# Another computed instruction order for the opening of a cross-attention and ReGLU kernel

## Chip, cores, metric

One core of one Trainium2 chip. The metric is device time of the core in microseconds (us), over several executions.

## The reference

```python
def _attn_ref(x, state):                  # x (8,8,512,64), state (8,8,32,64)
    scale = 1.0 / np.sqrt(D)
    a = softmax(scale * x @ state^T);   xread = a @ state
    a2 = softmax(scale * state @ x^T);  sread = a2 @ x
    return np.concatenate([xread, sread], axis=2)

def _moe_ref(x, w_gate, w_val, w_out):    # on 8 x (512 + 32) = 4352 rows of 512
    return (np.maximum(x @ w_gate, 0.0) * (x @ w_val)) @ w_out      # 512 -> 1536 -> 512
```

(The two softmaxes are written out in the original.) The output is (4352, 512) in float32; the kernel multiplies in bf16.

## The kernel before

The kernel never forms `xread`. It multiplies each batch's 32 state rows with both weight matrices (`U`, "state products") and the normalised attention, transposed (`ANS`), with `U`. The state products are *column-tiled*: each of their matmuls has the shape 64x32 in the profile's lines, where the others have 128x128. A *visit* is a group of them between whole ones. The program gives every group of matmuls one of eight PSUM banks, which is free again when ScalarE or VectorE has copied or used what is in it. Per batch the 1536 gate and value columns are 12 *slices* of 128 columns, four 512-column matmuls each. ScalarE takes the relu of a slice's gate half, VectorE multiplies it with the value half, and 12 *output pieces* of four matmuls follow.

```python
def c_unit(b, lo, n):                 # state products of n columns, gate and value
    ps = held["c", b, lo] = [bank("upc")[:, 0:2 * n]... for kc in range(NK)]
    for w in range(2):                # w 0: gate weights, 1: value weights
        u_mm([p[:, w] for p in ps], b, w, lo, n)    # eight 64x32 matmuls
def gv(b, jf):                        # one slice: 2 banks, 4 matmuls
    held["gv", b, jf] = [bank("gv_ps"), bank("gv_ps")], hsb[b][:, jf], S
    for w in range(2):
        for kc in range(NK):
            gv_mm(held["gv", b, jf][0], b, jf, w, kc)   # U x ANS
```

The order of the opening is a string of words. It covers batches 0 and 1, the preparation of batch 2 and the first four slices of batch 2. A word is a step with its arguments; digits after `@` are the PSUM banks; `.act`, `.dve`, `.pool` name the engine. Each engine gets its instructions in the order of the words:

```python
for word in program.split():
    word, _, banks = word.partition("@")
    given.extend(int(n) for n in banks)
    name, *args = word.split(".")
    steps[name](*(int(v) if v.isdigit() else v for v in args))
# then the steady loop:
for g in range(first, NF * (B + 1)):      # first = 2 * 12 + 4
    gv / relu / mult / an output piece, and the units hung on g
```

The words that matter: `spin` filler matmuls on TensorE; `xT`, `xT2` transposes of the input; `sc`, `ex`, `nr`, `nx` scores, exponential (ScalarE), row sums and scaling (VectorE); `aT`, `ao` transposes of the attention (`kc` 0 and 1) and their copies into `ANS`; `c`, `co` state products and their copies into `U`; `u`, `uo` the same 512 columns at a time; `gv`, `re`, `mu` a slice, its relu, its multiply; `o` an output piece; `sr`, `sn` the state read (`a2 @ x`); `dw`, `dx`, `ds`, `do`, `df` loads, `xn` casts, `xp` padded copies, all issued on GpSimd's queue.

The softmax here doesn't subtract the row's maximum and nothing guards it: scores larger than these inputs give would overflow.

## Time and profile before

| | before |
|---|---|
| time, median of 3 runs | 224.15 us (223.98 to 224.34) |
| span of the profiled run | 221.9 us |
| TensorE busy | 96% |
| products of columns 256 to 511: value half starts | 16.10 us, after a wait for weights |
| products of columns 512 to 767 start | 19.04 us |
| first slice of the steady loop starts | 55.72 us |

How to read it: TensorE is nearly full, so time is to be had only where TensorE stands before the steady loop. The last three rows cut the run into three stretches. A change in one stretch shows as a shift of the next mark; if the distance between two marks is the same in two kernels, nothing happened between them. The lines behind the rows are in the prediction.

Some matmul records are missing (x1930 of 1959 on the page before), so "x7" of an eight-matmul group can be a lost record. I compare starts of groups.

### The profile page before, as it was taken

The page shows a single profiled execution, that of the slowest core. Times are in us where ns is not written, and L with a number is a line of the kernel's source. Part 1 is how long each engine was busy: PE and PEld are TensorE (multiplying, and loading weights), DVE is VectorE, ACT ScalarE, POOL GpSimd, SP SyncE. Part 2 cuts the span into 40 slices and gives each one's busy share as a digit, 9 for nine tenths or more (in the row PEclk, how much of TensorE's full clock was granted, in tenths as well). Part 3 has the DMA queues.
Part 4 walks back from the last instruction along what each step waited for, and adds up shares of the span by engine and source line. Part 5 has one row for each costly group of instructions (what it writes and reads, how often), then busy time and mean ns, then how long its engine had stood idle before and what let it go on. Part 6 is the DMA issues. An engine that isn't in the chain of part 4 may idle for free.

```text
span 221.9 us, 4820 instructions
## 1 busy us (share of the span) xinstructions
PE 213.5 (96%) x1930; PEld 106.1 (48%) x1959; DVE 131.0 (59%) x233; ACT 123.3 (56%) x233; POOL 48.9 (22%) x54
## 2 busy tenths in 40 slices
PE   7989999999999999999999999999999999999994
PEld 3544454444544444444444444444444445666544
DVE  3489988965786568664867378646875433222100
ACT  4688788752567555574466456645655444222222
POOL 8867754300603343015000700000000000000000
PEclk9999999999999999999999999999999999999999
DMA  6999999062055862771169114511311112222332
GB/s 155 179 195 196 201 240 284 30 154 84 0 136 200 159 219 75 164 237 52 49 142 282 53 47 98 101 43 47 95 50 47 47 49 50 50 47 54 91 95 95
DMA packets 37879, 25.48 MB, mean 115 GB/s; under 512 B 18944, under 2 KB 33280, under 8 KB 37856
## 3 DMA queue, kind: packets, MB, share of 16 engines
q1 hardware_dynamic: 24992, 16.85, 27.5%
q0 software_dynamic: 11968, 7.47, 21.7%
q10 hardware_dynamic: 896, 0.85, 1.3%
q8 instruction: 15, 0.25, 0.5%
q14 instruction: 8, 0.07, 0.1%
HBM read 18.35 MB, written 8.91 MB: 123 GB/s over the span
## 4 chain that ended last, share of the span: by engine, by line
PE 83%; DMA 12%; POOL 2%; issue 2%; DVE 0%; POOLq 0%; DVEq 0%
PE o_ps L353 38%; PE gv_ps L316 31%; DMA st_f<-in_state_dram 5%; PE gv_ps L333 5%; PE up L291 4%; DMA wv_sb<-in_moe_w_val_dram 4%; DMA xb<-in_x_dram 3%; PE sc_ps L200 1%; PE o_ps L382 1%; PE sr_ps L264 1%; POOL st_b L124 1%; POOL xb L415 0%; PE stT_ps L129 0%; POOL xb L423 0%; PE aT_ps L235 0%
## 5 line engine op out<-in xcount | busy, mean ns | idle before, releaser
L316 PE MATMUL gv_ps<-ans,U 128*128 128x512 bf16 x372 | 93.6, 379 | 1.0 <-ACT ans L249 0.3
L353 PE MATMUL o_ps<-wo_sb,h_sb 128*128 128x512 bf16 x358 | 92.0, 379 | 1.7 <-issue 1.6
L340 ACT ACTIVATE g_sb<-gv_ps 128x512 bf16<-128x512 f32 (+1 forms) x108 | 62.7, 580 | 50.2 <-PE gv_ps L316 37.5
L344 DVE TENSOR_TENSOR h_sb<-gv_ps,g_sb 128x512 bf16<-128x512 f32 x96 | 64.8, 688 | 41.5 <-ACT g_sb L340 40.7
L316 PEld LDWEIGHTS <-U 128*128 128x128 bf16 x384 | 36.0, 98 | 40.7 <-issue 0.9
L353 PEld LDWEIGHTS <-h_sb 128*128 128x128 bf16 x372 | 35.3, 98 | 40.0 <-issue 1.6
L361 ACT COPY o_sb<-o_ps 128x512 f32<-128x512 f32 x29 | 17.1, 590 | 16.2 <-PE o_ps L353 16.2
L301 ACT CAST U<-up 128x512 bf16<-128x512 f32 x37 | 19.2, 594 | 11.1 <-PE up L291 11.1
L301 DVE CAST U<-up 128x512 bf16<-128x512 f32 x35 | 22.1, 683 | 2.3 <-PE up L291 1.9
L142 POOL CAST xb<-xf 128x1024 bf16<-128x1024 f32 x10 | 10.1, 1042 | 55.6 <-DMA xf<-in_x_dram 55.6
L256 POOL COPY xa<-xb 128x2048 bf16<-128x2048 bf16 (+1 forms) x9 | 15.6, 1750 | 12.9 <-issue 12.7
L213 DVE TENSOR_REDUCE cs<-e_sn 128x16 f32<-128x512 bf16 x16 | 10.8, 678 | 8.9 <-ACT e_sn L207 8.9
L344 DVE TENSOR_TENSOR hs_sb<-gv_ps,g_sb 128x256 bf16<-128x256 f32 x12 | 5.1, 425 | 15.3 <-PE gv_ps L333 10.5
L207 ACT ACTIVATE e_sn<-sc_ps 128x512 bf16<-128x512 f32 x16 | 9.7, 604 | 4.5 <-PE sc_ps L200 4.4
L219 DVE TENSOR_TENSOR a_sn<-e_sn,rc 128x512 bf16<-128x512 bf16 x16 | 11.1, 707 | 0.3
L291 PEld LDWEIGHTS <-stT 64*32 64x32 bf16 x512 | 6.0, 90 | 10.0 <-issue 8.7
L311 ACT CAST U<-upc 128x512 bf16<-128x512 f32 (+1 forms) x18 | 8.7, 542 | 1.5 <-PE upc L291 1.5
L291 PE MATMUL up<-wg_sb,stT 64*32 64x512 bf16 x144 | 7.5, 381 | 0.0
L200 PEld LDWEIGHTS <-xT 128*128 128x128 bf16 x128 | 5.6, 98 | 3.7 <-ACT xT L177 0.5
L333 PE MATMUL gv_ps<-br,wg_sb 128*128 128x256 bf16 x48 | 7.2, 273 | 0.1
L333 PE MATMUL gv_ps<-br,wv_sb 128*128 128x256 bf16 x48 | 7.2, 273 | 0.0
L291 PE MATMUL up<-wv_sb,stT 64*32 64x512 bf16 x144 | 7.1, 380 | 0.0
(65 smaller groups left out, 124.0 us busy)
## 6 DMA issues: line engine op xcount, KB each, us to landing
out_dram<-o_sb SPq DMA_DIRECT2D x26, 256.0 KB, 2.4
xf<-in_x_dram SPq DMA_DIRECT2D x4, 1024.0 KB, 6.1
wo_sb<-in_moe_w_out_dram POOLq DMA_DIRECT2D x2, 768.0 KB, 14.4
wg_sb<-in_moe_w_gate_dram POOLq DMA_DIRECT2D x5, 256.0 KB, 9.0
wv_sb<-in_moe_w_val_dram POOLq DMA_DIRECT2D x5, 256.0 KB, 9.7
out_dram<-o_sb SPq DMA_DIRECT2D x10, 128.0 KB, 2.4
xf<-in_x_dram POOLq DMA_DIRECT2D x1, 1024.0 KB, 15.3
xb<-in_x_dram POOLq DMA_DIRECT2D x3, 256.0 KB, 6.1
```

Source lines behind the costliest of these rows:

```text
L142: copy[eng](out=xb[b][:, :, hs].rearrange("p c h d -> p h c d"), in_=xf[b][:, hs])
L213: nc.vector.reduce_sum(out=cs, in_=e_v, axis=AX.X)
L219: {"dve": nc.vector, "pool": nc.gpsimd}[eng].tensor_tensor(out=by_pair(a_sn[b], jp).rearrange("p r (j n) -> p r j n", n=Ns), in0=e_v, in1= ...
L256: nc.gpsimd.tensor_copy(out=v[:, hs:hs + src.shape[1]], in_=src)
L291: nc.tensor.matmul(dst[parity][32 * j:32 * j + 32], stT[r:r + 64, b, j, 32 * parity:32 * parity + 32], wsb[r:r + 64, j, lo:lo + n], start= ...
L301: copy[eng](out=U[b][:, w, kc, lo:lo + 512], in_=held["u", b, w, lo][kc])
L316: nc.tensor.matmul(ps[w], U[b][:, w, kc, f0:f0 + 128], ANS[b][:, kc].rearrange("p c t -> p (c t)"), start=(kc == 0), stop=(kc == NK - 1))
L333: nc.tensor.matmul(ps[w][:, 0:nt], wsb[:, j, f0:f0 + 128], br[:, j].rearrange("p b n -> p (b n)"), start=(j == 0), stop=(j == NJ - 1))
L340: nc.scalar.activation(out=g_sb[:, 0:n], in_=ps[0][:, 0:n], func=AF.Relu)
L344: nc.vector.tensor_tensor(out=dst, in0=ps[1][:, 0:n], in1=held["g", b, jf][:, 0:n], op=ALU.mult)
L353: nc.tensor.matmul(held["o", b, tsub], src[:, jf, tsub * 128:(tsub + 1) * 128], wo_sb[:, jf], start=(jf == 0), stop=(jf == NF - 1))
L361: copy[eng](out=o_sb, in_=held["o", b, tsub])
```

## The change

Its intent: an order for the first 28 slices whose plan includes the first two steady slices and the slowing of VectorE's scaling where GpSimd copies at the same time (in the trace of before one took 1.12 us at 82.14, beside a GpSimd cast, and the next 0.69 at 86.08). The work is the same; the filler matmuls are placed differently (6, 4, 2, 2, 1 become 7, 1, 2, 2, 2, 1). ScalarE does 40 of the movable copies and conversions instead of 35, VectorE 23 instead of 28. The first output bank of the steady loop changes (`"o": 0` becomes 1). The rest is order and bank numbers; the core, with cuts:

```diff
 # around the columns 256 to 767 (copies and loads cut)
-gv.0.0@50 … nr.1.0 … gv.0.1@42 … nx.1.1 nx.1.0
-c.0.256.256@17 c.1.256.256@65 … aT.1.0@3 aT.1.1@4 … ao.1.0.dve gv.0.2@71 ao.1.1.dve
-… gv.1.0@36 … c.1.512.256@45 c.0.512.256@27
+gv.0.0@14 … nx.1.0 … c.1.128.128@65 nx.1.1 gv.0.1@20 … aT.1.1@7 … aT.1.0@1 ao.1.1.act
+c.0.256.256@36 ao.1.0.dve c.1.256.256@54 … gv.1.1@21
+… gv.1.0@73 … c.1.512.256@05 c.0.512.256@62
 # first half of the scaling ahead of the second sum; copies from VectorE to ScalarE
-nr.0.0 … nr.0.1 … nx.0.0 …   co.1.0.128.0.dve  co.0.0.128.0.dve  ao.0.1.dve
+nr.0.0 … nx.0.0 … nr.0.1 …   co.1.0.128.0.act  co.0.0.128.0.act  ao.0.1.act
 # the state reads of batches 0 and 1
-… o.0.9@7 mu.2.3 sr.0@4 sr.1@5 sn.0 sn.1 xp.2 xp.3          (the end of the program)
+… u.2.0.1024@05 u.2.1.512@34 … sr.0@1 sr.1@2 … sn.0 u.2.0.0@50 sn.1 xp.2 xp.3 …
```

So the transposes of batch 1's attention go ahead of the products of columns 256 to 511, and the slice after those products is one of batch 1 (`gv.1.1`), where it was `gv.0.2`.

More of the change, by code (lines that the diff above doesn't have):

```diff
@@ L77 @@
     copy = {"act": nc.scalar.copy, "dve": nc.vector.tensor_copy, "pool": nc.gpsimd.tensor_copy}
-    given, turn = [], {"r": 0, "o": 0}
+    given, turn = [], {"r": 0, "o": 1}
     def bank(name, kind="r"):
@@ L444 @@
     program = """
-    dx.1.0.2 dx.1.1.2 stc.0.0.act stc.0.1.dve xc.0.0.act dw.0.0.128 spin.6 stT.0@5 xT.0.0@0 xc.0.1.dve dw.1.0.128 on
-    sto.0.dve xT.0.1@4 xo.0.0.dve dw.0.128.128 xo.0.1.act dw.1.128.128 dw.0.256.256 spin.4 xT.0.3@2 dw.1.256.256
-    xT.0.2@3 xo.0.3.dve sc.0.0@1 xo.0.2.act ex.0.0 sc.0.1@6 dw.0.512.256 xT2.1.0@5 ex.0.1 nr.0.0 xo2.1.0.act
-    dw.1.512.256 spin.2 xT2.1.1@0 nr.0.1 xo2.1.1.act sc.1.0@4 dw.0.768.256 nx.0.0 dw.1.768.256 ex.1.0 spin.2
-    c.1.0.128@23 nx.0.1 sc.1.1@1 co.1.0.128.1.act c.0.0.128@65 co.1.0.128.0.dve dw.0.1024.256 aT.0.1@0 ex.1.1
@@ L450 @@
-    co.0.0.128.0.dve aT.0.0@4 co.0.0.128.1.act ao.0.1.dve dw.1.1024.256 ao.0.0.act spin.1 c.1.128.128@32 nr.1.1
-    c.0.128.128@16 co.1.128.128.1.act gv.0.0@50 co.0.128.128.0.act nr.1.0 co.0.128.128.1.act dw.0.1280.256 re.0.0
-    gv.0.1@42 co.1.128.128.0.act nx.1.1 re.0.1 nx.1.0 dw.1.1280.256 c.0.256.256@17 c.1.256.256@65 co.0.256.256.1.act
-    co.0.256.256.0.dve aT.1.0@3 aT.1.1@4 co.1.256.256.0.act ao.1.0.dve gv.0.2@71 dx.2.0.1 ao.1.1.dve
-    co.1.256.256.1.act mu.0.1 re.0.2 gv.1.0@36 mu.0.0 ds re.1.0 mu.0.2 c.1.512.256@45 c.0.512.256@27
@@ L455 @@
-    co.1.512.256.0.act co.1.512.256.1.dve gv.1.1@03 co.0.512.256.1.act do.0.6 co.0.512.256.0.dve re.1.1 gv.1.4@14
-    mu.1.0 xp.0 re.1.4 gv.1.3@57 mu.1.1 re.1.3 mu.1.4 gv.0.5@20 mu.1.3 do.6.12 re.0.5 gv.0.3@61 mu.0.5 xp.1 re.0.3
-    c.0.768.256@35 c.0.1024.256@47 mu.0.3 co.0.768.256.1.act gv.1.2@20 co.0.1024.256.1.act co.0.768.256.0.dve df.3
-    re.1.2 gv.0.4@61 co.0.1024.256.0.dve re.0.4 mu.1.2 gv.1.5@57 mu.0.4 re.1.5 gv.0.9@32 mu.1.5 re.0.9 gv.0.8@46
-    mu.0.9 re.0.8 c.1.1280.256@01 c.0.1280.256@57 mu.0.8 co.1.1280.256.1.act xT2.2.1@3 co.0.1280.256.1.act
@@ L460 @@
-    co.1.1280.256.0.dve xT2.2.0@2 stc.1.0.pool co.0.1280.256.0.act c.1.768.256@46 xo2.2.1.dve stc.1.1.pool
-    c.1.1024.256@17 xo2.2.0.act stc.3.0.pool gv.1.10@05 co.1.768.256.0.dve stc.2.0.pool co.1.768.256.1.dve
-    co.1.1024.256.1.act stc.2.1.pool stT.1@3 gv.1.11@42 stc.3.1.pool re.1.10 sto.1.dve co.1.1024.256.0.act mu.1.10
-    gv.0.11@76 re.1.11 re.0.11 mu.1.11 gv.1.7@30 mu.0.11 re.1.7 gv.1.9@15 mu.1.7 re.1.9 sc.2.0@4 gv.0.7@72 mu.1.9
-    ex.2.0 re.0.7 nr.2.0 gv.0.6@36 re.0.6 mu.0.7 gv.0.10@01 mu.0.6 re.0.10 u.2.0.0@45 u.2.1.512@73 nx.2.0
@@ L465 @@
-    uo.2.0.0.1.act u.2.0.512@20 o.0.0@6 mu.0.10 uo.2.0.512.1.act uo.2.1.512.0.act uo.2.0.0.0.dve sc.2.1@5 o.0.1
-    uo.2.0.512.0.act xn.3 uo.2.1.512.1.dve ex.2.1 u.2.1.1024@01 nr.2.1 u.2.1.0@42 uo.2.1.1024.0.act u.2.0.1024@35
-    o.0.2 uo.2.1.0.1.act uo.2.0.1024.1.dve uo.2.1.0.0.act o.0.3@7 nx.2.1 of.0.0.dve aT.2.1@0 gv.1.8@25
-    uo.2.1.1024.1.dve ao.2.1.act re.1.8 uo.2.0.1024.0.dve aT.2.0@4 o.0.4 ao.2.0.dve mu.1.8 gv.2.0@01 re.2.0 o.0.5
-    mu.2.0 gv.2.2@23 of.0.1.act re.2.2 gv.1.6@45 mu.2.2 re.1.6 o.0.6@6 mu.1.6 o.0.7 o.0.8 gv.2.1@01 of.0.2.dve re.2.1
@@ L470 @@
-    gv.2.3@23 mu.2.1 re.2.3 o.0.9@7 mu.2.3 sr.0@4 sr.1@5 sn.0 sn.1 xp.2 xp.3
+    dx.1.0.2 dx.1.1.2 stc.0.0.act stc.0.1.act xc.0.0.dve dw.0.0.128 spin.7 stT.0@4 xc.0.1.act dw.1.0.128 on xT.0.0@2
+    sto.0.dve xT.0.1@5 xo.0.0.dve dw.0.128.128 xo.0.1.dve dw.1.128.128 spin.1 sc.0.0@3 dw.0.256.256 ex.0.0 xT.0.2@0
+    xT.0.3@1 xo.0.2.dve dw.1.256.256 xo.0.3.act nr.0.0 spin.2 sc.0.1@6 dw.0.512.256 xT2.1.0@4 ex.0.1 nx.0.0
+    xo2.1.0.act nr.0.1 dw.1.512.256 spin.2 xT2.1.1@2 xo2.1.1.dve sc.1.0@5 dw.0.768.256 ex.1.0 nx.0.1 dw.1.768.256
@@ new lines @@
+    spin.2 c.0.0.128@30 sc.1.1@1 co.0.0.128.0.act nr.1.0 aT.0.1@6 co.0.0.128.1.act dw.0.1024.256 aT.0.0@4 ex.1.1
+    ao.0.0.dve ao.0.1.act dw.1.1024.256 spin.1 c.0.128.128@25 c.1.0.128@30 nr.1.1 co.0.128.128.1.act gv.0.0@14
+    co.0.128.128.0.act co.1.0.128.1.act nx.1.0 re.0.0 dw.0.1280.256 c.1.128.128@65 nx.1.1 gv.0.1@20 co.1.0.128.0.act
+    co.1.128.128.0.act mu.0.0 co.1.128.128.1.act aT.1.1@7 re.0.1 dw.1.1280.256 aT.1.0@1 ao.1.1.act c.0.256.256@36
+    ao.1.0.dve c.1.256.256@54 mu.0.1 co.0.256.256.0.act gv.1.1@21 dx.2.0.1 co.1.256.256.0.act co.0.256.256.1.dve
@@ new lines @@
+    re.1.1 gv.1.0@73 co.1.256.256.1.act mu.1.1 ds re.1.0 c.1.512.256@05 c.0.512.256@62 co.1.512.256.1.dve
+    co.1.512.256.0.act gv.1.2@41 co.0.512.256.1.act mu.1.0 do.0.6 co.0.512.256.0.act gv.0.3@70 re.1.2 xp.1 gv.1.5@52
+    re.0.3 mu.1.2 re.1.5 mu.0.3 gv.0.4@36 mu.1.5 re.0.4 xp.0 c.1.768.256@47 c.0.768.256@15 mu.0.4 co.1.768.256.0.act
+    gv.0.2@03 co.0.768.256.0.act co.1.768.256.1.dve re.0.2 gv.0.5@26 do.6.12 co.0.768.256.1.act mu.0.2 gv.1.7@41 df.3
+    re.0.5 re.1.7 mu.0.5 gv.0.7@70 mu.1.7 re.0.7 gv.1.3@53 mu.0.7 re.1.3 gv.1.4@24 mu.1.3 re.1.4 gv.1.6@61 mu.1.4
@@ new lines @@
+    re.1.6 c.1.1280.256@70 c.0.1280.256@53 mu.1.6 co.1.1280.256.0.act c.1.1024.256@24 stc.1.0.pool xT2.2.0@6
+    co.0.1280.256.0.act co.1.1024.256.0.dve xT2.2.1@1 co.0.1280.256.1.act co.1.1024.256.1.dve stc.1.1.pool
+    c.0.1024.256@75 xo2.2.1.act gv.0.10@23 co.1.1280.256.1.dve stc.3.1.pool co.0.1024.256.1.dve re.0.10 gv.1.9@40
+    co.0.1024.256.0.act xo2.2.0.dve stc.2.0.pool re.1.9 gv.0.6@12 mu.0.10 stc.3.0.pool re.0.6 mu.1.9 gv.0.11@57 mu.0.6
+    stc.2.1.pool re.0.11 gv.0.8@64 mu.0.11 re.0.8 stT.1@3 gv.1.10@10 mu.0.8 sto.1.act re.1.10 sc.2.0@2 o.0.0@7 ex.2.0
@@ new lines @@
+    mu.1.10 nr.2.0 sc.2.1@5 gv.0.9@34 ex.2.1 re.0.9 nx.2.0 o.0.1 mu.0.9 gv.1.11@12 nr.2.1 xn.3 re.1.11 o.0.2 mu.1.11
+    o.0.3@6 nx.2.1 of.0.0.act u.2.0.1024@05 u.2.1.512@34 uo.2.0.1024.0.dve uo.2.0.1024.1.act sr.0@1 sr.1@2
+    uo.2.1.512.1.act sn.0 u.2.0.0@50 sn.1 xp.2 xp.3 o.0.4 uo.2.0.0.0.act uo.2.0.0.1.dve aT.2.1@4 uo.2.1.512.0.dve
+    o.0.5 ao.2.1.act o.0.6@7 of.0.1.act u.2.1.0@12 u.2.0.512@50 uo.2.1.0.0.act uo.2.1.0.1.dve u.2.1.1024@34 o.0.7
+    uo.2.1.1024.0.act uo.2.1.1024.1.dve uo.2.0.512.0.act gv.1.8@12 uo.2.0.512.1.dve re.1.8 aT.2.0@3 o.0.8 mu.1.8
@@ L471 @@
+    ao.2.0.dve o.0.9@6 of.0.2.act gv.2.0@45 re.2.0 gv.2.2@01 mu.2.0 re.2.2 gv.2.1@23 mu.2.2 re.2.1 gv.2.3@45 mu.2.1
+    re.2.3 mu.2.3
     """
```

## The prediction

> **What bounds the kernel now.** I read the page first, then the list of TensorE's own waits, then TensorE in order of time over the first 56 us, then GpSimd and VectorE in order of time, last the chain that ended last.
>
> The page's first part, busy time and share of the span:
>
> ```profile
> PE 213.5 (96%) x1930; PEld 106.1 (48%) x1959; DVE 131.0 (59%) x233; ACT 123.3 (56%) x233; POOL 48.9 (22%) x54
> ```
>
> TensorE is near full, no other engine passes 59%. What is left to win is TensorE time lost before the steady loop, since the diff changes the opening program and the parity of the first output bank, nothing else. The chain gives the steady loop's price: the same place of three successive batches, start and duration.
>
> ```profile
> 80.74 0.59 PE gv_ps L316 x2
> ...
> 104.16 0.59 PE gv_ps L316 x2
> ...
> 127.57 0.59 PE gv_ps L316 x2
> ```
>
> A batch takes 104.16 - 80.74 = 23.42 us and again 23.41. Its TensorE work: 24 groups of four 512-column matmuls (12 gate/value slices, 12 output pieces) at 0.864 us, from the start-to-start of neighbouring groups in the chain (20.7), six column-tiled state products at 0.22 (1.3), scores, transpose and state read about 0.9: 22.9. So a steady batch loses some 0.5 us, fixed by the loop, which is not touched. The first, longer batch (55.72 to 80.31 in the timeline, 24.6 us) has three more state-read transposes, one more state read and two state transposes, about 1.0 us of extra work: 23.4 + 1.0 = 24.4. Thus at most 0.2 us is to be had in the first steady slices.
>
> TensorE's waits of the whole run (us in total, times, longest):
>
> ```profile
> PE warm_ps L435 <- DVE hs_sb L399: 1.2, 1, 1.2
> PE upc L291 <- DMA wv_sb<-in_moe_w_val_dram: 0.4, 1, 0.4
> PE sc_ps L200 <- ACT xT L177: 0.3, 1, 0.3
> PE gv_ps L316 <- ACT ans L249: 0.3, 1, 0.3
> PE stT_ps L129 <- DVE st_b L124: 0.2, 1, 0.2
> ```
>
> All are before 17 us and each under half a microsecond after the first. TensorE there, in order of time (start, duration, what, and in brackets the idle time before):
>
> ```profile
> 13.62 1.89 PE L316 MATMUL gv_ps<-ans,U 128*128 128x512 bf16 x8 [0.26 <-ACT ans L249]
> 15.43 0.30 PE L291 MATMUL upc<-wg_sb,stT 64*32 64x256 bf16 x8
> 16.10 0.30 PE L291 MATMUL upc<-wv_sb,stT 64*32 64x256 bf16 x8 [0.36 <-DMA wv_sb<-in_moe_w_val_dram]
> ...
> 16.55 0.62 PE L235 MATMUL aT_ps<-id,a_sn 128*128 128x128 bf16 x8
> 17.21 1.90 PE L316 MATMUL gv_ps<-ans,U 128*128 128x512 bf16 x7
> 19.04 0.30 PE L291 MATMUL upc<-wg_sb,stT 64*32 64x256 bf16 x8
> ```
>
> The first two slices end at 15.4, the products of columns 256 to 511 stand until their value weights land at 16.1, then the transposes of batch 1's attention and two slices run, and the products of columns 512 to 767 start at 19.04. They did not wait there: their value weights had landed at 10.09 + 8.45 = 18.54, by the chain:
>
> ```profile
> 10.09 8.45 DMA wv_sb<-in_moe_w_val_dram
> 18.82 11.42 DMA st_f<-in_state_dram
> ```
>
> So the two arrivals 16.1 and 18.5 are floors for any order, and before is 0.5 us above the second. From 19.04 to the first steady slice at 55.72 is 36.7 us. The work in it: 24 slices and 10 output pieces at 0.864 (29.4), eight 256-column products at 0.23 (1.8), six 512-column ones at 0.22 (1.3), transposes, scores and state reads about 2.8 (each read from the timeline as distances of starts): 35.3. The missing 1.4 us are mostly at each change between full and column-tiled matmuls: the pair at 19.04 holds 0.46 us of work, the next slice starts at 19.60, and its five slices take until 24.02 (4.42, against 5 x 0.864 = 4.32). Hence about 0.2 us a visit, and seven visits.
>
> [...]the page's mean of 379 ns is the length of overlapping records and I count starts. [...]the early filler matmuls start 0.42 to 0.43 us apart[...]. The trace has one such case, in the steady loop:
>
> ```profile
> 82.14 1.12 DVE L219 TENSOR_TENSOR a_sn<-e_sn,rc 128x512 bf16<-128x512 bf16 x1
> 86.08 0.69 DVE L219 TENSOR_TENSOR a_sn<-e_sn,rc 128x512 bf16<-128x512 bf16 x1
> ...
> 80.70 2.03 POOL L142 CAST xb<-xf 128x1024 bf16<-128x1024 f32 x2 [6.83 <-DMA xf<-in_x_dram]
> ```
>
> It costs VectorE 1.12 - 0.69 = 0.43 us, and TensorE nothing: the batch spacing above spans it.
>
> **The change part by part.**
> 1. Fillers: 15 become 13, and the first scores product moves ahead of the input's second half. Fillers stand only where TensorE would wait, so this is worth about 0 by itself. ScalarE now makes both state halves (0.4 later for the second), VectorE the first head pair; seven fillers (7 x 0.427 from 1.18 = 4.2) cover that.
> 2. Scaling of the first half moves ahead of the second sum on VectorE, and the first softmax no longer ends in two scalings in a row (1.22 us for two). Against that the copy of batch 1's transposed half (0.68) goes to VectorE before the last scaling, and its input lands only at 9.8. I add up: transposes to 10.4, copy to 11.1, scaling to 11.8, transposes, then copies of ANS by about 13.1. First slice at about 13.1 against 13.36: 0.2 to 0.3 us earlier.
> 3. Two products (columns 0 to 127 and 128 to 255 of batch 1) move behind or between the slices, and the transposes of batch 1's attention before the wait for weights instead of after it. The 0.45 us of those transposes thereby lie in the wait that ends at 16.1. Then products (0.46 with about 0.1 after), two slices of batch 1 (1.73): TensorE arrives at the columns 512 at about 18.4, and the floor 18.54 (+ 0.04, as at 16.06 to 16.10) binds. They end at about 18.95 against 19.49: 0.5 us won. This is the main term; the 0.25 us of item 2 is inside it, not added. Slices done by then are four in both.
> 4. After that the work is identical. The state reads of batches 0 and 1 move between state products, and the products are in six visits where there were seven: about 0.2 us won. The 0.16 us wait of the slice at 31.37 on a copy may go too.
> 5. New tight places, by adding relu (0.6), multiply (0.69) and about 0.1 to 0.2 us each of hand-over: the product of columns 1024 for batch 1 takes banks of a slice two earlier (0.1 to 0.2), the transpose after it (0.1), the state product after the state reads needs a bank that VectorE frees behind the scaling of batch 2, which may meet GpSimd's cast (0 to 0.3), and the first slice of batch 2 waits for its copy (0 to 0.1). Together 0.2 to 0.6 us lost; I take 0.4.
> 6. GpSimd's two padded copies (3.74 us at 55.67 before) no longer wait for state reads at the very end, and leave the first scalings of the steady loop alone. Those took 0.69 in before too, so nothing is won on the path.
>
> Sum: -0.5 - 0.2 - 0.1 + 0.4 = -0.4 us. 224.15 - 0.4 = 223.75.
>
> **Rivals.** (a) The order is tight all along and the stalls of item 5 do not come: 0.8 to 1.0 us faster, 223.2. For it: the order was computed from durations; against it: the plan assigns 40 copies to ScalarE where there were 35, and ScalarE must finish all in the slots computed. (b) A delay in the opening (ScalarE's longer queue[...]) makes batch 1's attention late, TensorE reaches the columns 512 at 19 or later, and the bank waits add up: 0 to 0.6 us slower, 224.4. For it: ScalarE has eight copies and relus between 12 and 16 us, adjacent in its queue, at 0.26 and 0.5 us each, so it has under 1 us of slack. Against it: the waits for weights at 16.1 and 18.5 absorb up to 0.5 us of it. (c) A transfer moves: the input of batch 2 or the state lands later since GpSimd's own instructions shift. The weights are all issued in the same order and the floors are GpSimd's queue, so I give it little; it would cost a microsecond at most.
>
> **Range and chances.** The most that can be won is the 0.5 us at the floor, the 1.4 us of changes and waits up to 55.7, and 0.2 us in the loop: 2.1 us, under 1%. So 2% faster (4.5 us) is out of reach, and 2% slower would need a stall far above any that I find. The runs of before span 0.36 us. Range 223.0 to 224.5.
>
> **What would show it.** First slice at about 13.1; columns 512 starting at 18.4 to 18.7 with a short wait on the value weights; the first steady slice at about 55.3 instead of 55.72; batches of 23.42 us after that. I am wrong if the second arrival is not what the columns 512 wait for, if TensorE has waits over 0.3 us after 20 us, or if the steady batches change their length.

"One such case" stands for a VectorE scaling beside a GpSimd cast, as the lines below it show. The 0.427 us of item 1 is the step of the early fillers in the trace of before (one starts at 2.00, the next at 2.43); a later 512-column matmul takes 0.864/4 = 0.216.

Three things in it need a correction. 13.36 is where TensorE begins to wait for the copy of ANS; the first slice itself starts 0.26 us later, at 13.62. The number of fillers does not change: both programs have 15, and both traces have 15 weight loads for them (two of their matmul records are lost in before). And the list of TensorE's waits leaves out three lines. One is the wait of 0.16 us at 31.37 that item 4 names, so not all waits are before 17 us; the others (1.6 us in ten pieces before output pieces, 0.2 before a filler) end on nothing that the profile shows and are absent from the trace of after that has all its matmul records, so they may be lost records.

## The result and the profile after

| | before | after |
|---|---|---|
| time, median of 4 runs | 224.16 us (223.98 to 224.34) | 223.12 us (222.88 to 223.50) |
| span of the profiled run | 221.9 | 221.7 |

The ratio is 0.9955, with a 95% interval of 0.9938 to 0.9972. Ratios here are the mean time of one kernel's fast runs over that of the other's in the same rounds, so not quite the ratio of the medians. By the 2% rule this is "same"; it is 1.0 us faster, and the interval lies clear of 1. A second measurement of each order on another chip job (first experiment below) gives four traces, two per order.

The page of the changed kernel, busy time:

```profile
PE 216.0 (97%) x1959; PEld 106.3 (48%) x1959; DVE 130.5 (59%) x228; ACT 124.8 (56%) x238; POOL 49.4 (22%) x54
```

The five instructions that left VectorE (233 to 228) are on ScalarE (233 to 238). TensorE's busy time cannot be compared, since this trace has all 1959 matmuls and the other has not. TensorE's waits of the changed kernel (us in total, times, longest):

```profile
PE warm_ps L435 <- DVE hs_sb L399: 1.2, 1, 1.2
PE xT_ps L173 <- DMA xb<-in_x_dram: 1.0, 1, 1.0
PE sc_ps L200 <- DVE xT L177: 0.2, 1, 0.2
```

The waits for value weights, for ANS and for the state transpose are gone; a wait for the input has come, before 8 us. TensorE of the changed kernel in order of time (start, duration, what):

```profile
13.79 1.05 PE L316 MATMUL gv_ps<-ans,U 128*128 128x512 bf16 x4
...
15.89 0.61 PE L235 MATMUL aT_ps<-id,a_sn 128*128 128x128 bf16 x8
16.43 0.30 PE L291 MATMUL upc<-wg_sb,stT 64*32 64x256 bf16 x8
16.55 0.29 PE L291 MATMUL upc<-wv_sb,stT 64*32 64x256 bf16 x8
...
17.02 1.90 PE L316 MATMUL gv_ps<-ans,U 128*128 128x512 bf16 x8
18.85 0.30 PE L291 MATMUL upc<-wg_sb,stT 64*32 64x256 bf16 x8
```

The transposes are over when the products begin, and the slices follow those at once: from the value half to the next products 18.85 - 16.55 = 2.30 us. Before, it is 19.04 - 16.10 = 2.94. The first slice is not earlier (13.79 against 13.62).

The marks of all four traces, us:

| | before | before, again | after | after, again |
|---|---|---|---|---|
| first slice | 13.62 | 13.65 | 13.79 | 13.53 |
| value half of columns 256 | 16.10 | 16.48 | 16.55 | 16.27 |
| its weights have landed | 16.06 | 16.45 | 16.29 | 16.02 |
| columns 512 start | 19.04 | 19.43 | 18.85 | 18.57 |
| first steady slice | 55.72 | 56.28 | 55.53 | 55.08 |
| span | 221.9 | 222.5 | 221.7 | 221.3 |
| time of this run | 223.72 | 224.26 | 223.50 | 223.06 |

The landing is read from GpSimd, whose next load waits for it and starts 0.28 us after it (the chain in the prediction has the same 0.28 between 18.54 and 18.82). The first steady slice of the changed order is the fifth of a group, so 4 x 0.864 is added to the group's start, 52.07 and 51.62 (0.864 us is the step from one group of four 512-column matmuls to the next: twenty in a row take 4.32 from 52.23 in the chain of after). These are the two kernels' lines on GpSimd, before and then after:

```profile
16.34 0.74 POOL L110 DMA_DIRECT2D wv_sb<-in_moe_w_val_dram  x1 [1.23 <-DMA wv_sb<-in_moe_w_val_dram]
```

```profile
16.57 0.74 POOL L110 DMA_DIRECT2D wv_sb<-in_moe_w_val_dram  x1 [0.75 <-DMA wv_sb<-in_moe_w_val_dram]
```

Where the time went, means of two traces each:
- **Up to columns 512**: 19.235 - 18.71 = 0.52 us. The stretch from the value half is 0.64 shorter (2.94 and 2.95, against 2.30 and 2.30); the value half itself starts 0.12 later (16.41 against 16.29).
- **Columns 512 to the first steady slice**: 36.68 and 36.85 before, 36.68 and 36.51 after: 0.17 us.
- **The rest**: span less first steady slice is 166.18 and 166.22 before, 166.17 and 166.22 after: nothing.

Together 0.7 us, which is also the difference of the means of these four runs (223.99 and 223.28). The timed runs of both jobs say about 1.0, with an interval of about 0.35 either way; against the six runs of "before, again" in the same job, the six of "after, again" are 0.76 us faster in the mean (224.01 and 223.25). What is left of 0.3 lies within this scatter and is not explained further.

The middle stretch resolves into two small waits. In both traces of before a slice waits 0.16 us for a copy of batch 2's transposed input; "before, again" also waits at the state transposes:

```profile
31.75 0.81 PE L316 MATMUL gv_ps<-ans,U 128*128 128x512 bf16 x3 [0.16 <-DVE xT L189]
32.79 0.40 PE L129 MATMUL stT_ps<-id,st_b 128*128 128x128 bf16 x4 [0.22 <-DVE U L311]
```

Neither trace of after has these. Its first trace lost about 0.17 us to the late input of batch 2: the transposes began 30.62 - 30.12 = 0.50 us after the group before, in the second trace 30.18 - 29.85 = 0.33. Less these waits, all four stretches are 36.5 us. So the whole of the state reads' new place is worth nothing by itself, as the lines of the two state reads show, before and then after:

```profile
54.13 0.81 PE L353 MATMUL o_ps<-wo_sb,h_sb 128*128 128x512 bf16 x3
55.08 0.71 PE L264 MATMUL sr_ps<-xa,e_sn 128*32 128x65 bf16 x64
55.72 1.04 PE L316 MATMUL gv_ps<-ans,U 128*128 128x512 bf16 x3
```

```profile
43.36 0.40 PE L291 MATMUL up<-wv_sb,stT 64*32 64x512 bf16 x8
43.69 0.71 PE L264 MATMUL sr_ps<-xa,e_sn 128*32 128x65 bf16 x64
44.32 0.43 PE L291 MATMUL up<-wg_sb,stT 64*32 64x512 bf16 x8
```

Before, four matmuls (one record lost) end at 54.13 + 0.864 = 54.99, and the next slice starts at 55.72: 0.73 us for the two reads with both changes of tile shape. After, the product ends at 43.36 + 0.22 = 43.58 and the next starts at 44.32: 0.74. The shapes differ, 64x32 and 128x32, so going straight from one to the other cost as much here as going by a full matmul.

Last, the clash that the plan was to cover. VectorE's scaling in the changed kernel, and GpSimd's cast at that time:

```profile
42.32 1.30 DVE L219 TENSOR_TENSOR a_sn<-e_sn,rc 128x512 bf16<-128x512 bf16 x1
```

```profile
42.04 2.48 POOL L142 CAST xb<-xf 128x1024 bf16<-128x1024 f32 x2 [4.90 <-DMA xf<-in_x_dram]
```

The clash is there, longer than the one at 82.14 in before (1.12); the scaling that stands here at 42.32 took 0.67 in before, with no cast beside it. Its length depends on when it starts: in the traces it ends 0.53 to 0.55 us after the cast that it met (in before 83.26 against 82.73; here 43.62, after the first of the two casts). TensorE waits for it nowhere, and didn't before.

### The profile page after: what moved, and what is told of

Its sections match the earlier page's. It is cut to its first block, busy times and chain, and to the rows that moved or that the text cites. A ratio compares the mean times of both kernels' runs of the same rounds, so it can differ in the third digit from the quotient of the medians.

```text
span 221.7 us, 4851 instructions
## 1 busy us (share of the span) xinstructions
PE 216.0 (97%) x1959; PEld 106.3 (48%) x1959; DVE 130.5 (59%) x228; ACT 124.8 (56%) x238; POOL 49.4 (22%) x54
## 4 chain that ended last, share of the span: by engine, by line
PE 85%; DMA 12%; POOL 1%; issue 0%; DVE 0%; POOLq 0%; DVEq 0%
PE o_ps L353 39%; PE gv_ps L316 32%; DMA xb<-in_x_dram 9%; PE gv_ps L333 5%; PE up L291 4%; DMA wg_sb<-in_moe_w_gate_dram 4%; PE sr_ps L264 1%; PE sc_ps L200 1%; PE o_ps L382 1%; PE xT_ps L186 0%; POOL xb L415 0%; PE stT_ps L129 0%; PE aT_ps L235 0%; PE srT_ps L277 0%; PE upc L291 0%
## 5 line engine op out<-in xcount | busy, mean ns | idle before, releaser
L353 PE MATMUL o_ps<-wo_sb,h_sb 128*128 128x512 bf16 x372 | 94.8, 379 | 0.0
L361 ACT COPY o_sb<-o_ps 128x512 f32<-128x512 f32 x31 | 18.3, 590 | 17.4 <-PE o_ps L353 17.4
L142 POOL CAST xb<-xf 128x1024 bf16<-128x1024 f32 x10 | 10.6, 1088 | 66.4 <-DMA xf<-in_x_dram 45.4
L301 DVE CAST U<-up 128x512 bf16<-128x512 f32 x36 | 22.7, 684 | 4.1 <-PE up L291 3.7
L219 DVE TENSOR_TENSOR a_sn<-e_sn,rc 128x512 bf16<-128x512 bf16 x16 | 12.4, 778 | 0.4
L311 ACT CAST U<-upc 128x512 bf16<-128x512 f32 (+1 forms) x21 | 10.1, 570 | 0.5 <-PE upc L291 0.4
```

Of the source, the lines that this page charges most:

```text
L142: copy[eng](out=xb[b][:, :, hs].rearrange("p c h d -> p h c d"), in_=xf[b][:, hs])
L219: {"dve": nc.vector, "pool": nc.gpsimd}[eng].tensor_tensor(out=by_pair(a_sn[b], jp).rearrange("p r (j n) -> p r j n", n=Ns), in0=e_v, in1= ...
L301: copy[eng](out=U[b][:, w, kc, lo:lo + 512], in_=held["u", b, w, lo][kc])
L353: nc.tensor.matmul(held["o", b, tsub], src[:, jf, tsub * 128:(tsub + 1) * 128], wo_sb[:, jf], start=(jf == 0), stop=(jf == NF - 1))
L361: copy[eng](out=o_sb, in_=held["o", b, tsub])
```

## The experiments

Every kernel ran in five rounds beside the kernel before; three jobs, in which before had medians of 224.29, 223.99 and 224.24 us (11 runs each). All gave a correct result.

**Theory H** ("head"): the time is won before the columns 512, because the transposes and their copies no longer stand between the arrival of the weights and those products. **Rival T** ("tail"): it is won in the order after them (state reads, fewer changes of tile shape). **Rival S**: it is slack; the arrivals of weights set the marks, whatever the opening does.

### Each order once more

No edit.

> The kernel before, unchanged, for the noise of the method and a second trace. Theory D (arrival luck): the trace shows the input of heads 4 to 7 (the first transfer on GpSimd's queue) landing at another time than the 7.0 us of the first trace, and the columns-512 products start as much later or earlier as it did; ratio 1.000 +- 0.001. If instead the landing is 7.0 again, the late landing of the changed kernel (7.8) belongs to the change.

> The changed kernel, unchanged. Ratio 0.9955 again (0.9945 to 0.9965). Theory D: the landing is not always 7.8; if it is 7.0 to 7.3 here, TensorE shows waits on the weights at about 16.1 and 18.5 and the columns-512 products start at 18.6.

Before again: 223.85 us, ratio 0.9991 (0.9975 to 1.0008). After again: 223.22 us, 0.9957 (0.9942 to 0.9973). The gain repeats. The two traces are in the table above. TensorE of before, again:

```profile
16.48 0.30 PE L291 MATMUL upc<-wv_sb,stT 64*32 64x256 bf16 x8 [0.71 <-DMA wv_sb<-in_moe_w_val_dram]
...
19.43 0.30 PE L291 MATMUL upc<-wg_sb,stT 64*32 64x256 bf16 x8
```

The weights came 0.39 us later than in the first trace, and everything after them too: in before the products of columns 512 stand 2.94 us behind that arrival. In neither trace of after did TensorE stand at those weights; it came 0.25 us after them.

Theory D, luck with the arrival of the input, is not borne out. In "before, again" the transposes of the late input start 0.08 us later than in the first trace (7.12, 7.04), but columns 512 are 0.39 later. In "after, again" they start at 7.26, and columns 512 at 18.57 as expected, but without the waits on weights that D asked for.

### Head of one, tail of the other

```diff
 # head_after_tail_before: after's program up to c.0.512.256, then before's
+<after: dx.1.0.2 … gv.1.1 … gv.1.0 … c.1.512.256 c.0.512.256>
+<before's rest, with its gv.1.1 replaced by gv.0.2, banks renumbered>
 # head_before_tail_after: the other way round
+<before: dx.1.0.2 … gv.0.2 … gv.1.0 … c.1.512.256 c.0.512.256>
+<after's rest, with its gv.0.2 replaced by gv.1.1, banks renumbered>
```

> The changed kernel's order up to the columns-512 products, then the old order (slice 2 of batch 0 and slice 1 of batch 1 exchanged, since the two heads did one each; banks renamed). Theory H (the gain is made before the columns-512 products and only carried after): 0.8 to 1.0 us faster than before, as the changed kernel. Rival T (the gain is made after it, in the visits to column-tiled products and the bank waits): 0 to 0.2 us.

> The old order up to the columns-512 products, then the changed one. Theory H: within 0.2 us of before. Rival T: 0.8 to 1.0 us faster.

The tail of after behind the head of before: 224.12 us, 0.9998 (0.9981 to 1.0016), columns 512 at 19.02. The tail alone gains nothing measurable, against rival T. A wait of 0.25 us at the seam is inside it.

The head of after with the tail of before was to gain. It did not: 224.56 us, 1.0023 (1.0006 to 1.0040). Its trace has two waits that neither parent has:

```profile
18.78 0.30 PE L291 MATMUL upc<-wg_sb,stT 64*32 64x256 bf16 x8 [0.42 <-ACT U L311]
...
21.23 2.97 PE L316 MATMUL gv_ps<-ans,U 128*128 128x512 bf16 x13 [0.84 <-DVE h_sb L344]
```

Without the first it would have been at columns 512 at 18.36. The banks and the copies at the seam fit neither tail, and 1.26 us of waits hide what the head won. As a test of H this run failed; it shows that an order of this tightness can't be cut and joined freely.

### The transposes back behind the products

```diff
 # after
-aT.1.1@7 re.0.1 dw.1.1280.256 aT.1.0@1 ao.1.1.act c.0.256.256@36 ao.1.0.dve c.1.256.256@54
+re.0.1 dw.1.1280.256 c.0.256.256@36 c.1.256.256@54 aT.1.1@7 aT.1.0@1 ao.1.1.act ao.1.0.dve
```

> The changed kernel with the transposes of batch 1's attention (and their two copies) put behind the pair of columns-256 products instead of ahead of it; all else the same. Theory W (the gain is that the transposes lie in the wait for weights and that a slice which needs no new columns comes next): TensorE idles some 0.4 us before the products, the next slice starts 0.5 to 0.7 us later, the kernel gives back 0.5 to 0.7 us of its 1.0 (ratio 0.998 to 0.999). Rival R (the gain is made elsewhere, in the opening or after 19 us): within 0.2 us of the changed kernel (0.995 to 0.9965).

224.29 us, 1.0012 (0.9995 to 1.0030): the whole gain is given back, some 1.2 us. TensorE:

```profile
16.38 0.30 PE L291 MATMUL upc<-wv_sb,stT 64*32 64x256 bf16 x8 [0.44 <-DMA wv_sb<-in_moe_w_val_dram]
...
16.84 0.62 PE L235 MATMUL aT_ps<-id,a_sn 128*128 128x128 bf16 x8
17.98 1.90 PE L316 MATMUL gv_ps<-ans,U 128*128 128x512 bf16 x8 [0.52 <-DVE ans L249]
19.80 0.30 PE L291 MATMUL upc<-wg_sb,stT 64*32 64x256 bf16 x8
```

The wait for the value weights is back, and the transposes are back on the path (0.46 us from 16.84 to where the wait begins, 17.98 - 0.52). The 0.52 more is a wait that before does not have: there a slice of batch 0 stands between the transposes and the first use of their copies, here a slice of batch 1 uses them at once. H's step is shown, with some 0.6 of the 1.2, as expected; the other half was not expected and belongs to this mixture of the two orders.

### Two copies back on VectorE

```diff
 # after
-co.0.0.128.0.act
+co.0.0.128.0.dve
-co.1.0.128.0.act            (behind gv.0.1)
+co.1.0.128.0.dve            (behind co.1.0.128.1.act, ahead of nx.1.0)
```

> The changed kernel with two of the copies that it moved from VectorE to ScalarE (columns 0 to 127 of batch 0 and of batch 1, first half) put back on VectorE, ahead of batch 1's sums and scalings. Theory V (batch 1's attention is ready in the wait only because VectorE was relieved): the last scaling of batch 1 ends about 0.7 us later, the transposes with it, 0.3 to 0.6 us lost. Rival: ScalarE was the tighter engine, and the kernel is the same or faster.

223.58 us, 0.9975 (0.9956 to 0.9995): about 0.4 us of the gain is lost. Its TensorE, then VectorE's last scaling of batch 1:

```profile
13.75 1.04 PE L316 MATMUL gv_ps<-ans,U 128*128 128x512 bf16 x4 [0.31 <-DVE ans L249]
...
16.10 0.62 PE L235 MATMUL aT_ps<-id,a_sn 128*128 128x128 bf16 x8
...
19.07 0.30 PE L291 MATMUL upc<-wg_sb,stT 64*32 64x256 bf16 x8
```

```profile
14.76 1.28 DVE L219 TENSOR_TENSOR a_sn<-e_sn,rc 128x512 bf16<-128x512 bf16 x2
```

The scaling ends at 16.04, where it ended at 14.20 + 1.22 = 15.42 in after, again, and at 14.49 + 1.22 = 15.71 in after. The transposes start right behind it, at 16.10, and columns 512 come at 19.07, 0.50 and 0.22 later than in those traces. From the first slice to columns 512 it is 5.32 us, against 5.04 and 5.06; the first slice, too, now waits, 0.31 us for VectorE's copy of ANS. So the timing of the early transposes rests in part on the copies that moved to ScalarE; with these two back, some 0.6 us of the gain stays.

### Four fillers more ahead of the first slice

```diff
 # fillers_after: ahead of c.0.128.128;   fillers_before: ahead of c.1.128.128
-spin.1
+spin.5
```

> The changed kernel with four more filler matmuls (4 x 0.216 = 0.86 us of TensorE time) ahead of the first slice. If its opening is on the path (no wait for weights left after it): 0.5 to 0.9 us slower than the changed kernel, ratio 0.9975 to 1.0. If the arrival of the weights at 16.1 and 18.5 is what binds it, as the prediction said: under 0.3 us slower (0.9955 to 0.997).

> The kernel before with four more filler matmuls (0.86 us) at the same place. It waits 0.4 to 0.7 us for the columns-256 weights, so if the landing binds it, the first part of the delay is absorbed: 0.1 to 0.4 us slower (ratio 1.0005 to 1.002). If not: 0.6 to 0.9 us (1.003 to 1.004).

Four fillers are 0.86 us of TensorE (4 x 0.216; in the trace with before, the five ahead of the first slice take 1.24 us, of which the last record is 0.38: four steps of 0.215). In after:

```profile
14.15 1.04 PE L316 MATMUL gv_ps<-ans,U 128*128 128x512 bf16 x4
...
19.19 0.30 PE L291 MATMUL upc<-wg_sb,stT 64*32 64x256 bf16 x8
```

Columns 512 come at 19.19 against 18.57 in after, again (and 18.85 in after, whose input came later), the span is 221.9 against 221.3, the time 223.94 us, 0.9998 (0.9976 to 1.0021): 0.62 us later by that trace, 0.9 by the timed runs. The opening is on the path; what was absorbed, 0.24, was absorbed ahead of the first slice. From there to columns 512 it takes 5.04 us, as in after (5.06 and 5.04): no wait for weights stands in between. That is against rival S. In before the columns 512 come at 19.11, against 19.04 and 19.43; the time is 224.25 us, 1.0016 (0.9993 to 1.0039), and the wait for weights is gone from the list. There the same fillers vanish in that wait and in the one for ANS. S is true of before, not of after: in before columns 512 follow the value half by 2.94 to 2.96 us in four traces, whenever the weights let it start; in after they follow the first slice.

### The moves put into before, one and then two

```diff
 # before_transposes_early: before with
-c.0.256.256@17 c.1.256.256@65 … aT.1.0@3 aT.1.1@4 … ao.1.0.dve gv.0.2@71 … ao.1.1.dve
+aT.1.0@3 aT.1.1@4 ao.1.0.dve ao.1.1.dve … c.0.256.256@17 c.1.256.256@65 … gv.0.2@71
 # before_two_moves: the same, and gv.1.1 (with re, mu) in the place of gv.0.2, gv.0.2 in
 # that of gv.1.1, banks renumbered
```

> The kernel before with batch 1's attention transposes (and their copies) put ahead of the columns-256 products, its slice order kept (slice 2 of batch 0 next, which needs the new columns). Theory W says that the transposes alone are not enough: the next slice waits for the copy of its new columns out of PSUM, as the trace of before showed (0.2 us), and VectorE finishes batch 1 only at about 15.9. Gain 0 to 0.3 us (ratio 0.9985 to 1.000), or a small loss through the two copies ahead on VectorE. Rival (the prediction's step, 0.45 us of transposes hidden): 0.45 us, ratio 0.998.

> The same, and slice 1 of batch 1 instead of slice 2 of batch 0 next, which needs no new columns (banks renamed so that no product waits for a multiply). VectorE still carries the copies. Theory W with V: the columns-512 products start at 18.8 to 19.0 where before has 19.04 to 19.43, so 0.3 to 0.6 us of the 1.0 is won (ratio 0.997 to 0.9987); the rest needs VectorE relieved. Rival: these two moves are all of it, ratio 0.9957.

The transposes alone: 224.43 us, 1.0013 (0.9992 to 1.0033).

```profile
16.04 0.62 PE L235 MATMUL aT_ps<-id,a_sn 128*128 128x128 bf16 x8 [0.48 <-DVE a_sn L219]
...
17.88 1.90 PE L316 MATMUL gv_ps<-ans,U 128*128 128x512 bf16 x7 [0.66 <-DVE U L311]
19.71 0.30 PE L291 MATMUL upc<-wg_sb,stT 64*32 64x256 bf16 x8
```

They wait 0.48 for the scaling, which ends at 15.9 in before's order. Then `gv.0.2` waits 0.66 for the copies of the columns just made, time that the transposes used to fill. With `gv.1.1` in its place that second wait is gone:

```profile
16.17 0.62 PE L235 MATMUL aT_ps<-id,a_sn 128*128 128x128 bf16 x8 [0.48 <-DVE a_sn L219]
...
19.11 0.30 PE L291 MATMUL upc<-wg_sb,stT 64*32 64x256 bf16 x8
...
21.86 1.46 PE L316 MATMUL gv_ps<-ans,U 128*128 128x512 bf16 x6 [1.14 <-DVE h_sb L344]
```

But the scaling is as late as ever, so columns 512 come no earlier than 19.11, and a multiply behind two copies in VectorE's queue then holds a bank for 1.14 us: 225.24 us, 1.0053 (1.0031 to 1.0075). I had expected 0.3 to 0.6 us of gain, and was wrong. The 1.14 us come from my numbering of the banks, which was to have no product wait for a multiply; without them the time would be about that of before (225.24 - 1.14 = 224.10). So neither the transposes alone nor these two moves won anything while VectorE kept the copies. That the three parts of the opening (copies to ScalarE, transposes forward, a slice that needs no new columns) are enough together is likely, but not shown: no run puts just these three into before, or the copies alone.

### The state reads back at the end

```diff
 # after
-sr.0@1 sr.1@2 … sn.0 … sn.1 xp.2 xp.3      (between the products u.2.1.512 and u.2.0.0)
+sr.0@1 sr.1@2 sn.0 sn.1 xp.2 xp.3           (behind of.0.2.act, ahead of gv.2.0)
```

> The changed kernel with the state reads of batches 0 and 1 (and GpSimd's two padded copies behind them) near the end of the opening again, between output piece 9 and the first slice of batch 2. The visit to column-tiled products that this adds costs 0.15 to 0.3 us between 19 and 55.5 us in the trace; ratio 0.9962 to 0.997. GpSimd's copies end at about 56 instead of 48; if their clash with the scaling mattered, batches of the steady loop get longer, which I do not expect (0.0).

223.84 us, 0.9985 (0.9965 to 1.0006): some 0.6 us lost, where 0.15 to 0.3 had been expected. The profiled run was the slowest of the six (224.76 us, mean clock 0.991, its opening a microsecond late), so only distances are read from it: columns 512 to first steady slice takes 37.25 us, where after has 36.51 and 36.68.

```profile
43.88 0.40 PE L291 MATMUL up<-wv_sb,stT 64*32 64x512 bf16 x8
44.80 0.48 PE L291 MATMUL up<-wg_sb,stT 64*32 64x512 bf16 x8 [0.52 <-ACT U L301]
...
52.69 0.71 PE L264 MATMUL sr_ps<-xa,e_sn 128*32 128x65 bf16 x64
53.33 3.84 PE L316 MATMUL gv_ps<-ans,U 128*128 128x512 bf16 x16
```

The third product would have started at 43.88 + 0.22 = 44.10; it starts at 44.80, when a copy has freed its bank. That 0.70 is the whole loss: the reads themselves cost the same at their old place. So in after the reads fill a wait that after's own order of products would have. In before another order of products has no such wait. The move is part of a consistent order, and no gain by itself.

### Fewer fillers: an attempt at a faster version

```diff
 # after
-spin.2            (ahead of c.0.0.128)
-spin.1            (ahead of c.0.128.128)
```

> The changed kernel without the last two groups of fillers (3 x 0.216 us) ahead of the first slice. They should stand where TensorE waits anyway: first slice 0 to 0.15 us earlier, and the columns-512 products no earlier than the landing of their weights at about 18.55, so 0 to 0.1 us gained (ratio 0.995 to 0.996). If it gains 0.3 us or more, the plan still had slack there.

223.49 us (223.16 to 225.23), 0.9984 (0.9955 to 1.0013): inconclusive in time, no gain in the trace.

```profile
16.31 0.30 PE L291 MATMUL upc<-wv_sb,stT 64*32 64x256 bf16 x8
...
18.60 0.30 PE L291 MATMUL upc<-wg_sb,stT 64*32 64x256 bf16 x8
```

TensorE now comes to the value weights at 16.14 and they are there at 16.27; columns 512 start at 18.60, as in after, again (18.57). In after the weights are there only 0.15 to 0.26 us before the work that needs them, so little more is to be had here by filling TensorE better; no version beat after.

## Why the prediction was right

The time, 223.12 against a predicted 223.75, lies in the range, but only just: its lower end was 223.0, and two of the four runs are below that. The gain is 1.0 us where 0.4 was expected. One of the signs that the prediction named for being wrong came true: the columns 512 do not wait for the second arrival. By its steps:

- **Bound and limit.** Right. Steady batches are 23.4 us in both kernels, and the rest of the run from the first steady slice is the same to 0.05 us.
- **Item 1, fillers worth 0.** The count was misread: there are 15 in both, at other places. Nothing shows by itself what their places are worth.
- **Item 2, first slice 0.2 to 0.3 earlier, at 13.1.** Wrong in the mark; what is won is 0.16 in the mean, within the scatter. Four traces with after's opening unedited to that point have 13.44 to 13.79, five with before's 13.62 to 13.85 (a fifth of after's opening, with slow early matmuls, 1.06 us for 16 input transposes that take 0.64 in after, at a mean clock of 0.991, has 14.45 and is left out). The sum ran from the input's arrival as before has it; in both traces of after the last input transposes start later (7.26 and 7.83, against 7.04 and 7.12). Over all traces it is 7.16 to 7.83 in eight with after's first words and 7.04 to 7.32 in six with before's. Why is open: the loads have the same order.
- **Item 3, 0.5 us at columns 512.** Right in size, 0.52, and in its working part: the transposes leave the stretch behind the weights. Wrong in what binds. I had TensorE at 18.4 waiting for the second arrival at 18.54. In after it comes by its own work: columns 512 start at 18.57 and 18.85, their value half 0.12 later, 0.15 after its weights in both traces. The gain per trace is 0.64 in the stretch (0.45 of transposes and some 0.2 of a hand-over of copied columns behind them, which I had not counted), less 0.12 at its start. Adding fillers shows that no floor protects this opening. That the size came out is partly luck: I had the start 0.25 early, where it is 0.12 late, and the hand-over of 0.2 was missing.
- **Item 4, 0.2 from state reads and fewer visits, 0.1 from a wait.** The wait of 0.16 is gone. The 0.2 is nothing: the reads with their two changes of shape took 0.73 in the old place and 0.74 in the new.
- **Item 5, 0.4 lost to new tight places.** This is the mis-sized term. No TensorE wait above 0.2 us follows 20 us in either trace of after. I had added up worst hand-overs one by one for places that the new order fills with other work; the third product of the state-read visit is one of them, and taking its filler away costs 0.70.
- **Item 6 and the clash.** Right: scaling of 1.30 us beside a cast, no TensorE wait.

So the sum should have read -0.5 - 0.1 with no plus: -0.6 to -0.7, what the traces have. Rival (a), "tight all along, 0.8 to 1.0", describes the timed result. Rival (b) was right that the opening has hardly any slack, wrong that it would be late in the usual run. A lower granted clock was seen once in a trace, that of the state reads put back: its page has 6 tenths in the slice from 5.6 to 11.1 us, where the pages of before and after have 9 throughout; the mean is 0.991, the first slice comes at 14.45. Two more of the 46 runs with after's opening have a mean clock of 0.991 or 0.992, and all three are 0.5 to 1.1 us slower than the other runs of their kernels; of 63 listed runs with before's opening none is below 0.998. Whether the fewer fillers before 8 us (8, where before has 10) have to do with it was not tested. Rival (c), a transfer that moves, cost 0.17 us once, in the first trace of after.

## What to carry to other kernels

Mark three or four points of the critical engine and compare distances between them; with two traces per kernel that resolved 0.2 us of 224, which the times alone could not. Put work that needs no new data ahead of an arrival, and behind the arrival only what the next step needs; but check the chain that makes the moved work ready, since moving it alone (or with one partner) won nothing here. When you guess new stalls in a computed order, look at what fills each gap before you add its worst case.

## What the traces show of the hardware

- 512-column matmuls in a stream of weight loads and matmuls start 0.864/4 = 0.216 us apart: twenty take 4.32 us from 52.23 in after.
- A visit of column-tiled products between full matmuls costs about 0.1 us on each side, for example in before: the slices from 17.21 are done at 17.21 + 2 x 0.864 = 18.94, 0.46 us of work starts at 19.04, the next slice at 19.60. Going from 64x32 to 128x32 tiles directly cost as much (0.74 us against 0.73 for the same two reads).
- A scaling of 0.67 to 0.69 us took 1.01 us (41.88 in after, again) to 1.54 us (81.93 in after) beside a GpSimd cast, by when it started, and ended 0.53 to 0.55 us after that cast. Where it came in the first cast of a pair (42.32 in after), the second cast took 1.50 us for 1.04, and the pair 2.48, where a pair with no scaling beside it takes 2.02 (from 40.98 in before).
- With one order of loads, the value weights of columns 256 landed at 16.06 and 16.45 in the two traces of before, and its time to the next mark went with them.
